# First row tiles loaded singly, their transposes evicted in halves, eleven dummy matmuls, D added on GpSimd, and a newly found order

## The chip, the cores and the metric

The kernel runs on one core of one Trainium2 chip. A core has five engines, each with its own queue of instructions: TensorE (PE in the profile; its weight loads are PEld), VectorE (DVE), ScalarE (ACT), GpSimd (POOL) and SyncE (SP), and 16 DMA engines that move data between the chip's memory and the core's two on-chip memories, SBUF and PSUM. TensorE writes only to PSUM; VectorE and ScalarE read it from there ("evict" it) into SBUF. The metric is the device time of one execution in microseconds (us), lower is better; a run's time is compared as a median over executions.

## What is computed

Inputs are bfloat16. The sequence has 2048 rows of 512 channels; the feed-forward width is 1792.

```
xn = layernorm(x)                                  # x = A_q, rows of 512
# branch A: a long convolution, written with FFTs in the reference
k_shift = 4-tap causal convolution of k along the rows
kv = k_shift * v
y  = causal convolution of kv with ssm_k, length 2048   # by FFT of length 4096
s  = xn * (y + kv * ssm_D)
# branch B: a gated feed-forward layer
h  = gelu(xn @ w_gate) * (xn @ w_up)
g  = silu(h @ w_down)
out = x + s * g
```

Since y + kv * D is the convolution of kv with a filter whose element 0 is larger by D, the kernel adds D to row 0 of the filter.

## The kernel before

**Tiling.** Row r of the sequence is tile t = r mod 16 at partition r div 16, so a tile is 128 x 512 and there are 16 of them, in four quarters q of four tiles. The feed-forward branch goes by quarters: normalise the four tiles (`ln`), transpose them (`xn_transpose`; quarter 0 on TensorE, the others by a transposing DMA), then for each of 14 column blocks m the gate and up matmuls (`unit`, four contraction steps each, 512 columns), GELU on ScalarE, the product on VectorE into HT, and then `down`. Blocks m = 0 and 1 of quarter 0 are cut further: their matmuls go tile by tile (128 columns), so that they can start when tile 0 is transposed.

**The convolution** is a two-stage FFT as matmuls. The filter's four pieces (Hn) are transposed on TensorE (L916) and evicted into HTr; stage 1 of the filter (L959) and of kv (L950) use half of the array's rows, two matmuls side by side ("packed"); the middle stage (L1028) uses sixteen 32 x 32 pieces of the array side by side; the results go through DRAM (ZH, ZK, ZI) to be rearranged. The inverse ends in the matmuls of L1278.

**The order.** All work is put down as tasks, numbered as they are added (`Sched.add`, helpers `op`, `load`). Each has one or two engines that could do it, a duration and what it depends on. `SEQ` is a list of all task numbers; a task is emitted in that order, on its first engine, or on its second where the number has a `b` behind it. The order was found beforehand with the planner's durations, and the planner's landing times of the loads stand in `LAND` (in ns). `Sched.run` goes through the list, gives buffers and PSUM banks to the tasks, and the emission then puts semaphore waits where they are needed (`Trk`). So within each engine's queue the order is that of `SEQ`, and an instruction that waits holds up all those behind it on its engine.

**The start.** SyncE issues the loads in the order of `ORDER` (helper L614): x in two halves of two tiles each (`load_x0`), the first gate and up weights, D, the filter, and so on. Meanwhile TensorE runs `N_WARM` dummy matmuls on a constant (`warm_up`). Statistics of each tile (L849, L850) go on VectorE, the variance plus epsilon (L859 on ScalarE or L860 on VectorE), the power -1/2 on GpSimd (L862), and the normalisation on VectorE (L871). TensorE transposes a normalised tile (L892, four matmuls against the identity) into one PSUM bank, and one 128 x 512 copy evicts it into xnT (helpers L632 on ScalarE, L635 on VectorE); then the gate matmuls (helper L641) can start. D is added to row 0 of the filter by one 1 x 512 VectorE operation (`h_fold`, L930), after the filter's first-half evictions and before stage 1 of tile pair 0.

Of the kernel before, what the change touches and what calls it, by code (L numbers as in the profile page):

```python
# [24 lines left out]
N_WARM = 13  # L25
ORDER = "x00 x01 w0 D0 h0 w1 h1 h2 h3 s0 k0 w2 x1 k1 k2 w3 d0 d1 v0 v1 k3 v2 v3 x2 x3"
SEQ = (
# [22 lines left out]
)  # L50
NF_BANKS = 4
ISSUE = 470.0
LAND = {"x0_0": 3800, "h0": 8050, "x0_1": 4900, "D": 6750, "wg0": 5850, "wu0": 6700, "h1": 12450, "wg1": 9600, "wu1": 11100, "h2": 13800, "h3": 15150, "sk": 17800, "kh1": 19200, "kh113": 19400, "kz": 10800, "k0": 20600, "wg2": 22500, "wu2": 24050, "x1": 25400, "k1": 26750, "k2": 28100, "wg3": 29650, "wu3": 31200, "wd0": 33450, "wd1": 35700, "v0": 37050, "v1": 38400, "k3": 39750, "v2": 41100, "v3": 42450}
W_XT, W_SW, W_BK, W_BH, W_ZI, W_BI, W_ZK, W_MI, W_G1 = 765000, 735000, 667000, 688000, 274000, 714000, 690000, 329000, 150000
NC_PAIRS = 4
SMALL = 1.15 * 262144
# [1308 lines left out]
```

## Time and profile before

| what | us |
|---|---|
| median of three runs | 189.29 (189.12 to 190.32) |
| the profiled execution | 189.28 |
| its span, first to last instruction | 187.5 |
| TensorE, VectorE, ScalarE, GpSimd busy in it | 182.2, 164.8, 140.0, 12.9 |

The span lacks 1.78 us of the profiled execution's own time; that part lies before the first and behind the last instruction. A group's line in the profile gives the source line, engine, operation, what is written from what, the shapes, the count, the busy time with the mean duration in ns, and the idle time before it with what ended that. A matmul's duration reaches from its start to the arrival of its last result, so matmuls of a stream overlap in the records: their pace is read from starts, or from the chain of waits, which merges them.

### The profile page before, as it was taken

What the parts mean: (1) busy time and instruction counts of PE and PEld (TensorE: products, weight loads), DVE (VectorE), ACT (ScalarE), POOL (GpSimd) and SP (SyncE); (2) the same over time, 40 slices, a digit from 0 to 9 for tenths busy, and PEclk for the clock granted to TensorE, in tenths of its full rate; (3) what the DMA queues carried; (4) which work ended last, traced back from release to release, by engine and by line L of the source; (5) the groups of instructions that cost most, each with busy time, mean ns of one, the idle gap of its engine ahead of it and who ended that gap; (6) DMA issues with size and microseconds to landing.
All of it is one profiled execution on the core that took longest, in us unless ns stands there. A gap on an engine that the chain in (4) does not pass through costs nothing.

```text
span 187.5 us, 3669 instructions
## 1 busy us (share of the span) xinstructions
PE 182.2 (97%) x1451; PEld 80.5 (43%) x1459; DVE 164.8 (88%) x249; ACT 140.0 (75%) x193; POOL 12.9 (7%) x26
## 2 busy tenths in 40 slices
PE   8899999999999999999999999999999999999993
PEld 3585443444334344334434433434333334445552
DVE  6897999999999999969459999998899994468995
ACT  3766697898698979888878779888887863144961
POOL 4502304100000000020200000000000000000000
PEclk9999999999999999999999999999999999999999
DMA  5999999999938695777999991869327056699226
GB/s 156 352 404 299 373 374 377 394 404 245 326 87 330 225 337 212 241 260 241 290 268 261 352 343 65 298 229 334 108 111 277 0 168 217 228 325 385 83 101 235
DMA packets 38502, 48.37 MB, mean 258 GB/s; under 512 B 9427, under 2 KB 28119, under 8 KB 38486
## 3 DMA queue, kind: packets, MB, share of 16 engines
q1 hardware_dynamic: 31958, 39.76, 64.1%
q10 hardware_dynamic: 6528, 8.39, 12.6%
q8 instruction: 11, 0.18, 0.5%
q14 instruction: 5, 0.04, 0.1%
HBM read 27.39 MB, written 14.68 MB: 224 GB/s over the span
## 4 chain that ended last, share of the span: by engine, by line
PE 91%; DVE 3%; DMA 2%; ACT 1%; issue 1%; POOL 0%
PE psall L641 71%; PE psall L1224 6%; PE psall L1028 6%; PE psall L950 2%; PE psall L959 2%; PE psall L916 2%; PE psall L1278 2%; DMA X<-in_A_q_dram 2%; ACT BO L632 1%; DVE stats L849 1%; DVE KAC L1005 1%; PE psall L892 0%; DVE XN L871 0%; DVE XN L965 0%; DVE HT L1203 0%
## 5 line engine op out<-in xcount | busy, mean ns | idle before, releaser
L641 PE MATMUL psall<-xnT,Wu 128*128 128x512 bf16 (+1 forms) x248 | 56.5, 359 | 0.0
L641 PE MATMUL psall<-xnT,Wg 128*128 128x512 bf16 (+1 forms) x248 | 55.8, 359 | 0.0
L1194 ACT ACTIVATE GE<-psall 128x512 bf16<-128x512 f32 x54 | 31.9, 606 | 13.6 <-PE psall L641 11.1
L641 PE MATMUL psall<-Wd,HT 128*128 128x512 bf16 (+1 forms) x174 | 38.3, 367 | 0.8 <-issue 0.6
L1203 DVE TENSOR_TENSOR HT<-psall,GE 128x512 bf16<-128x512 f32 x43 | 29.3, 682 | 7.8 <-PE psall L641 7.5
L641 PEld LDWEIGHTS psall<-xnT,Wu 128*128 128x128 bf16 x248 | 22.5, 98 | 26.1 <-issue 2.3
L641 PEld LDWEIGHTS psall<-xnT,Wg 128*128 128x128 bf16 x248 | 21.8, 98 | 26.0 <-issue 3.2
L632 ACT ACTIVATE BO<-psall 128x1024 bf16<-128x1024 f32 x20 | 19.9, 1022 | 9.4 <-PE psall L1278 4.8
L641 PEld LDWEIGHTS psall<-Wd,HT 128*128 128x128 bf16 x182 | 16.3, 98 | 21.2 <-issue 3.9
L1131 DVE TENSOR_TENSOR HSW<-KB,HSW 128x2048 bf16<-128x2048 bf16 x16 | 19.3, 1218 | 1.9 <-ACT KB L632 1.9
L632 ACT ACTIVATE HSW<-psall 128x1024 bf16<-128x1024 f32 x15 | 15.2, 1024 | 2.4 <-PE psall L1028 2.1
L632 ACT ACTIVATE KB<-psall 128x1024 bf16<-128x1024 f32 x15 | 14.6, 1026 | 0.8 <-PE psall L1028 0.8
L1011 DVE TENSOR_TENSOR KAC<-KAC,KTM 128x2048 bf16<-128x2048 bf16 x12 | 14.6, 1217 | 0.0
L1009 DVE TENSOR_TENSOR KTM<-KK,SKB 128x2048 bf16<-128x2048 bf16 x12 | 14.6, 1215 | 0.0
L632 ACT ACTIVATE AST<-psall 128x1024 bf16<-128x1024 f32 x12 | 12.1, 1032 | 0.9 <-PE psall L950 0.8
L1224 PE MATMUL psall<-Wd,HT 128*64 128x512 bf16 (+1 forms) x112 | 12.5, 366 | 0.0
L862 POOL TENSOR_TENSOR mv<-mv,NHALF 128x1 f32<-128x1 f32 (+1 forms) x7 | 7.3, 1049 | 68.6 <-DVE mv L850 48.0
L1235 ACT ACTIVATE G<-psall 128x512 bf16<-128x512 f32 x12 | 7.1, 597 | 6.3 <-PE psall L641 6.3
L849 DVE BATCH_NORM_STATS2 stats<-X 128x6 f32<-128x512 bf16 x16 | 10.5, 675 | 0.5 <-DMA X<-in_A_q_dram 0.5
L632 ACT ACTIVATE XN<-psall 128x1024 bf16<-128x1024 f32 x9 | 9.2, 1028 | 1.1 <-PE psall L959 1.0
L1237 DVE SCALAR_TENSOR_TENSOR G<-G,psall 128x512 bf16<-128x512 bf16 x12 | 7.9, 682 | 2.3 <-ACT G L1235 2.3
L1131 DVE TENSOR_TENSOR KB<-KB,HSW 128x2048 bf16<-128x2048 bf16 x8 | 9.7, 1219 | 0.1
(91 smaller groups left out, 178.3 us busy)
## 6 DMA issues: line engine op xcount, KB each, us to landing
BH<-ZH SPq DMA_DIRECT2D x8, 512.0 KB, 5.0
HSW<-HSW SPq DMA_DIRECT2D x16, 256.0 KB, 3.7
BK<-ZK SPq DMA_DIRECT2D x8, 512.0 KB, 5.9
ZI<-BO ACTq DMA_DIRECT2D x16, 256.0 KB, 2.8
BI<-ZI SPq DMA_DIRECT2D x8, 512.0 KB, 8.5
ZK<-AST SPq DMA_DIRECT2D x6, 512.0 KB, 2.9
ZH<-XN ACTq DMA_DIRECT2D x5, 512.0 KB, 4.3
Hn<-in_A_ssm_k_dram SPq DMA_DIRECT2D x4, 512.0 KB, 8.0
```

Of the source, the lines that this page charges most:

```text
L632: return h.activation(o, i, ACTF.Copy, scale=scale)
L641: return h.matmul(o, lhsT=l, rhs=r, start=st, stop=sp)
L849: t_stats[t] = op([("DVE", 670.0)], lambda e, h, t=t: h.bn_stats(stats[:, t, :], X[:, t, :]), r=[bX[q][t % 4]], w=[bst[t]], rr=[R_X[t]], w ...
L862: t_pw = op([("POOL", 2500.0 if q else 600.0)], lambda e, hd, ts=ts, n=n: hd.tensor_tensor(mv[:, ts, 3:4], mv[:, ts, 2:3], NHALF[:, 0:n, : ...
L1009: op([("DVE", dur)], lambda e, h, j=j, m=m: h.tensor_tensor(KTM[:, m.slot, :, :], kk(j), sk(j), ALU.mult), r=need + [bSKB[j], a], w=[m], r ...
L1011: op([("DVE", dur)], lambda e, h, m=m: h.tensor_tensor(KAC[:, a.slot, :, :], KAC[:, a.slot, :, :], KTM[:, m.slot, :, :], ALU.add), r=[m], ...
L1028: trk.op("PE", lambda h: h.matmul(ps(s, i)[b, :], lhsT=wt(col)[a, :], rhs=data(col)[a, :], start=n < 16, stop=n >= len(todo) - 16, tile_po ...
L1131: return hd.tensor_tensor(pair(KB, *(2 * DM * z for z in slots())) if to else x, k, x, ALU.mult)
L1194: op([("ACT", act(512))], lambda e, h: h.activation(GE[:, g.slot, :], bank(pg), ACTF.Gelu_apprx_tanh), r=[pg], w=[g], rr=lambda: R_bank(pg ...
L1203: op([("DVE", dve(512, 1))], lambda e, h: h.tensor_tensor(HT[:, q % 2, m, :], bank(pu), GE[:, g.slot, :], ALU.mult), r=[pu, g], w=[bHT[q][m]],
L1224: trk.op("PE", lambda h, m=m, i=i, c=c: h.matmul(pc()[c, :], lhsT=HT[:, q % 2, m, 128 * jt + 64 * i:128 * jt + 64 * i + 64], rhs=Wd[:, m, ...
L1237: op([("DVE", dve(512, 1))], lambda e, h, g=g, pc=pc: h.scalar_tensor_tensor(out=g, in0=g, scalar=1.0, in1=pc(), op0=ALU.add, op1=ALU.mult ...
```

## The change

Five things change together.

- The first load of x, two tiles at once, is split into two loads of one tile each; the second pair stays one load. `ORDER` has one entry more.
- The transposes of tiles 0 and 1 go to two PSUM banks each, two of the four 128-column pieces in each, and are evicted by two copies of 128 x 256, for which either engine can be chosen (`N_SPLIT = 2`). The matmuls that read a tile wait for both halves.
- There are 11 dummy matmuls instead of 13.
- D is added by GpSimd instead of VectorE.
- `SEQ` is a new order of all tasks (812 instead of 809: one load and two evictions more), with new choices of engines, and `LAND` and one planner duration (ScalarE's variance, 240 to 300) are new.

```diff
-N_WARM = 13
-ORDER = "x00 x01 w0 D0 h0 w1 h1 h2 h3 s0 k0 w2 x1 k1 k2 w3 d0 d1 v0 v1 k3 v2 v3 x2 x3"
+N_WARM = 11
+ORDER = "x00 x01 x02 w0 D0 h0 w1 h1 h2 h3 s0 k0 w2 x1 k1 k2 w3 d0 d1 v0 v1 k3 v2 v3 x2 x3"
 SEQ = (
...
-LAND = {"x0_0": 3800, "h0": 8050, "x0_1": 4900, "D": 6750, "wg0": 5850, "wu0": 6700,
...
+LAND = {"x0_0": 3450, "h0": 8200, "x0_1": 4300, "x0_2": 5100, "D": 6850, "wg0": 5900, "wu0": 6750,
...
+N_SPLIT = 2
...
         def load_x0(t):
-            ts = slice(*((0, 2), (2, 4))[t])
+            ts = slice(*((0, 1), (1, 2), (2, 4))[t])
...
-            pp = [B(f"psxn{q}_{j}", pX) for j in range(4)]
             for j in range(4):
...
+                pieces = [(0, 2), (2, 4)] if j < N_SPLIT else [(0, 4)]
+                pp = [B(f"psxn{q}_{j}" + "b" * (k0 > 0), pX) for k0, _ in pieces]
+
+                def tr(e, j=j, pieces=pieces, pp=pp):
+                    for (k0, k1), p in zip(pieces, pp):
+                        for kd in range(k0, k1):
+                            o = bank16(p)[:, 128 * (kd - k0):128 * (kd - k0 + 1)]
+                            trk.op("PE", lambda h, o=o, kd=kd: h.transpose(o, XN[:, 4 * q + j, 128 * kd:128 * (kd + 1)], ident[:]), r=[R_XN[4 * q + j], R_id], w=R_bank(p), accum=True)
+                S.add([("PE", 4 * 66.0)], tr, r=[bid, bXN[4 * q + j]], w=pp, lat=150.0)
+                for (k0, k1), p in zip(pieces, pp):
+                    def ev(e, h, j=j, k0=k0, k1=k1, p=p):
+                        return copy(e, h, xnT[:, q, j, k0:k1, :].rearrange("p k c -> p (k c)"), bank16(p)[:, 0:128 * (k1 - k0)])
+                    n = 128 * (k1 - k0)
...
-        h_fold = op([("DVE", 420.0)], lambda e, h: h.tensor_tensor(HT0, HT0, Drow[:], ALU.add),
+        h_fold = op([("POOL", 1200.0)], lambda e, h: h.tensor_tensor(HT0, HT0, Drow[:], ALU.add),
```

The start of the new order, as names (VectorE's tasks of the first tiles): statistics of tiles 0, 1, 3, normalise 0, normalise 1, the second half of tile 0's eviction, statistics of tile 2, the first half of tile 1's eviction, normalise 3, normalise 2. Before, they were: statistics 0 and 1, normalise 0, statistics 2, normalise 1, statistics 3, normalise 2, normalise 3. ScalarE now does the variance of tiles 0, 1 and 3 and two half evictions before it computes the sines of the table (`m_sin`); before, it did the variance of tile 0 and then `m_sin`. TensorE, after the dummies, transposes tiles 0 and 1 and then runs the eight groups of blocks m = 0 and 1 on them; before, it put block work on tile 0 between the transposes of tile 1 and those of the filter.

More of the change, by code (lines that the diff above doesn't have):

```diff
@@ L547, in build_kernel @@
         R_xnT = [[res(f"xnT{b}_{j}", xnT[:, b, j, :, :]) for j in range(4)] for b in range(2)]
+        R_xnT0 = [[res(f"xnT0_{j}_{k}", xnT[:, 0, j, 2 * k:2 * k + 2, :]) for k in range(2)] for j in range(N_SPLIT)]
         R_GE = [res(f"GE{j}", GE[:, j, :]) for j in range(3)]
@@ L650, in build_kernel @@
         bxnT = [[B(f"xnT{q}_{h}") for h in range(4 if q < 1 else 1)] for q in range(NQ)]
+        bxnT0 = [[B(f"xnT0_{j}" + "b" * k) for k in range(2)] for j in range(N_SPLIT)]
         bF1, bG1, bMF, bMI, bid, bSKB = B("F1"), B("G1"), B("TF"), [B(f"MI{i}") for i in range(2)], B("id"), [B(f"SKB{j}") for j in range(4)]
@@ L860, in var @@
                     return hd.tensor_scalar(mv[:, ts, 2:3], mv[:, ts, 1:2], LN_EPS, None, ALU.add)
-                t_var = op([("DVE", 180.0)] + ([] if q else [("ACT", 240.0)]), var, r=[bconst, bF1, *bm], w=[be], rr=rm + [R_ep], ww=rm)
+                t_var = op([("DVE", 180.0)] + ([] if q else [("ACT", 300.0)]), var, r=[bconst, bF1, *bm], w=[be], rr=rm + [R_ep], ww=rm)
                 t_pw = op([("POOL", 2500.0 if q else 600.0)], lambda e, hd, ts=ts, n=n: hd.tensor_tensor(mv[:, ts, 3:4], mv[:, ts, 2:3], NHALF[:, 0:n, :], ALU.pow),
@@ L886, in xn_transpose @@
                 return
-            pp = [B(f"psxn{q}_{j}", pX) for j in range(4)]
             for j in range(4):
-                def tr(e, j=j):
-                    for kd in range(KD):
-                        o = bank16(pp[j])[:, 128 * kd:128 * (kd + 1)]
-                        trk.op("PE", lambda h, o=o, kd=kd: h.transpose(o, XN[:, 4 * q + j, 128 * kd:128 * (kd + 1)], ident[:]), r=[R_XN[4 * q + j], R_id], w=R_bank(pp[j]), accum=True)
-                S.add([("PE", 4 * 66.0)], tr, r=[bid, bXN[4 * q + j]], w=[pp[j]], lat=150.0)
-            for j in range(4):
-                def ev(e, h, j=j):
-                    return copy(e, h, xnT[:, q, j, :, :].rearrange("p k c -> p (k c)"), bank16(pp[j])[:, 0:512])
-                xnT_tasks.append(op([("ACT", act(512)), ("DVE", dve(512, 2))], ev, r=[pp[j]], w=[bxnT[q][j]],
-                   rr=lambda j=j: R_bank(pp[j]), ww=[R_xnT[q][j]]))
+                pieces = [(0, 2), (2, 4)] if j < N_SPLIT else [(0, 4)]
[10 more added lines that the diff above has]
+                    n = 128 * (k1 - k0)
+                    xnT_tasks.append(op([("ACT", act(n)), ("DVE", dve(n, 2))], ev, r=[p], w=[bxnT[q][j]] if n == 512 else [bxnT0[j][k0 // 2]],
+                       rr=lambda p=p: R_bank(p), ww=[R_xnT[q][j]] if n == 512 else [R_xnT0[j][k0 // 2]]))
         d_out = []
@@ L1189, in unit @@
                 return
-            tg = S.add([("PE", pe(4))], half(pg, Wg, "g"), r=[bW["g"][ci]] + bxnT[q], w=[pg], lat=150.0)
-            tu = S.add([("PE", pe(4))], half(pu, Wu, "u"), r=[bW["u"][ci]] + bxnT[q], w=[pu], lat=150.0, after=[tg])
+            tg = S.add([("PE", pe(4))], half(pg, Wg, "g"), r=[bW["g"][ci]] + (bxnT[q] if q else [*bxnT[q][N_SPLIT:], *sum(bxnT0, [])]), w=[pg], lat=150.0)
+            tu = S.add([("PE", pe(4))], half(pu, Wu, "u"), r=[bW["u"][ci]] + (bxnT[q] if q else [*bxnT[q][N_SPLIT:], *sum(bxnT0, [])]), w=[pu], lat=150.0, after=[tg])
             gu_tasks[q] += [tg, tu]
```

4 lines of the change are left out of this document (2 added, 2 removed), and 44 rows, old and new, of the table SEQ.

## The prediction

> **What bounds the kernel now.** I read the first part of the page, the busy time by stretch, the chain of waits and TensorE's own waits, and last the timeline of the first 8 us.
>
> ```profile
> PE 182.2 (97%) x1451; PEld 80.5 (43%) x1459; DVE 164.8 (88%) x249; ACT 140.0 (75%) x193; POOL 12.9 (7%) x26
> ```
> ```profile
> core 0: us, PE busy (x) PEld busy (x) DVE busy (x) ACT busy (x) POOL busy (x), PEclk, DMA share, GB/s
> 0.00:6.30 6.30, 5.54 (x13) 1.75 (x13) 4.61 (x19) 3.10 (x5) 3.17 (x16) 1.00 0.67 206
> ...
> 20.00:24.00 4.00, 3.69 (x22) 1.79 (x19) 4.00 (x7) 2.21 (x4) 0.25 (x1) 1.00 1.08 385
> ...
> 40.00:100.00 60.00, 59.58 (x358) 23.75 (x359) 53.15 (x81) 50.88 (x71) 2.03 (x2) 1.00 0.84 260
> 100.00:146.00 46.00, 45.84 (x510) 18.20 (x510) 44.41 (x51) 38.49 (x51) 0.00 (x0) 1.00 0.68 235
> ...
> 184.00:187.50 3.50, 0.60 (x11) 0.42 (x8) 1.31 (x5) 0.55 (x2) 0.00 (x0) 0.93 0.55 186
> ```
> ```profile
> PE psall L641 <- PEq L1350: 0.8, 1, 0.8
> PE psall L641 <- issue: 0.6, 4, 0.2
> PE psall L892 <- DVE XN L871: 0.5, 1, 0.5
> PE psall L959 <- DVE HT L1203: 0.3, 1, 0.3
> ```
> In the second fence the columns are the length of the stretch and each engine's busy time in it; in the third, who waited for whom, the sum, the count and the longest. TensorE is busy in 97% of the span, and all its waits before the last matmul add up to 2.2 us: 0.8 before the program starts, 0.5 in front of the second tile's transposes, 0.3 in front of an L959 matmul, 0.6 without a cause. A busy TensorE need not be a full one, so the chain is read for its pace:
>
> ```profile
> 7.24 0.40 PE psall L892 x4
> 7.63 1.16 PE psall L641 x20
> ...
> 18.38 2.70 PE psall L641 x12
> ...
> 24.91 5.18 PE psall L641 x24
> ...
> 59.72 0.54 PE psall L950 x4
> ```
> Twenty-four 512-column matmuls in a row take 5.18 us, 0.216 each; twelve of them between two packed groups (L959 and L950 use half of the array's rows) take 2.70 and not 2.59, and four packed ones, two pairs side by side, 0.54 and not 0.43. So going into packed mode and out again costs 0.11 us each way. From 7.24 us on the chain is almost all TensorE. The kernel is bound by TensorE's work; only the start (the first 7.5 us), the number of mode changes, a few small waits, and the tail of 3 us can give time. VectorE stands right behind: full from 20 to 24 us, 44.41 of 46 us from 100 to 146.
>
> **The change, part by part.** The rows of the start:
>
> ```profile
> 0.72 0.87 SPq L614 DMA_DIRECT2D X<-in_A_q_dram  x2
> ...
> 1.64 0.43 SPq L614 DMA_DIRECT2D Wg<-in_B_w_gate_dram  x1
> ...
> 3.92 0.69 DVE L849 BATCH_NORM_STATS2 stats<-X 128x6 f32<-128x512 bf16 x1 [0.52 <-DMA X<-in_A_q_dram]
> ...
> 4.65 0.18 DVE L850 BATCH_NORM_AGGREGATE mv<-stats 128x2 f32<-128x6 f32 x1
> ...
> 4.86 0.29 ACT L859 ACTIVATE mv<-mv,EPSC 128x1 f32<-128x1 f32 x1 [1.88 <-DVE mv L850]
> ...
> 5.24 1.21 POOL L862 TENSOR_TENSOR mv<-mv,NHALF 128x1 f32<-128x1 f32 x2 [2.29 <-ACT mv L859]
> ...
> 5.85 0.41 DVE L871 TENSOR_SCALAR XN<-X,mv 128x512 bf16<-128x512 bf16 x1
> 6.18 0.69 DVE L849 BATCH_NORM_STATS2 stats<-X 128x6 f32<-128x512 bf16 x1
> ...
> 6.32 0.40 PE L892 MATMUL psall<-ident,XN 128*128 128x128 bf16 x4
> ...
> 6.78 0.40 DVE L871 TENSOR_SCALAR XN<-X,mv 128x512 bf16<-128x512 bf16 x1
> ...
> 6.87 0.58 ACT L632 ACTIVATE xnT<-psall 128x512 bf16<-128x512 bf16 x1
> ...
> 7.50 0.40 PE L641 MATMUL psall<-xnT,Wg 128*128 128x128 bf16 x4
> ```
> *Loads.* The first transfer halves to 128 KB. Its landing is bounded by 0 (the time is latency) and 0.59 us earlier (131 KB at the rate below); I take 0.35, landing at 3.55, which is also the step in the planner's own table (3800 to 3450). One load more is one issue more on SP's queue, 0.43 us (half of 0.87), and every load behind it is issued that much later.
>
> ```profile
> 1.50:2.50 1.00, 1.00 (x4) 0.37 (x3) 0.90 (x7) 0.51 (x1) 0.89 (x6) 1.00 0.64 221
> ```
> ```profile
> Wg<-in_B_w_gate_dram SPq DMA_DIRECT2D x1, 256.0 KB, 4.0
> ```
> The first gate weights, issued at 1.64, land 4.0 us later, at 5.6; they are first used at 7.50, so 0.43 is covered with 1.4 to spare. Without that cover it would cost its 0.43 in full.
>
> *Normalisation of the first two tiles.* Read against the order in which the program adds its tasks, the lists of numbers are lists of names. VectorE's new order is: statistics of tiles 0, 1 and 3, normalise 0, normalise 1, half evictions. With the durations above (an operation starts up to 0.08 before the last one's end, as 6.18 against 5.85 + 0.41): statistics of tile 0 from 3.57 to 4.26, aggregate to 4.48, statistics of tile 1 from 4.42 to 5.10, of tile 3 from 5.22 to 5.90, normalise 0 from 5.84. That is where it is now: the 0.35 won is spent on the statistics moved in front. Normalise 1 follows at 6.30, not 6.78 (aggregate 1 done at 5.30, ScalarE 0.29, GpSimd 0.58, rounding and hand-overs 0.1). So both tiles' transposes lie before 7.2, in time that TensorE has free.
>
> *Evictions in halves.*
> ```profile
> L635 DVE COPY HTr<-psall 128x1024 bf16<-128x1024 bf16 x4 | 2.8, 689 | 1.1 <-PE psall L916 1.0
> ...
> L632 ACT ACTIVATE HTr<-psall 128x1024 bf16<-128x1024 bf16 x2 | 2.0, 1021 | 0.1
> ...
> L632 ACT ACTIVATE xnT<-psall 128x512 bf16<-128x512 bf16 x3 | 1.8, 593 | 0.2 <-PE psall L892 0.2
> ...
> L635 DVE COPY xnT<-psall 128x512 bf16<-128x512 bf16 x1 | 0.4, 425 | 0.1
> ```
> From 1024 to 512 columns ScalarE saves 0.43 and VectorE 0.26, so a half of 256 takes about 0.38 and 0.29. Tile 0's halves run side by side: ScalarE's, the later, ends at 6.87 + 0.38 = 7.25, and the first gate matmul starts at 7.30 instead of 7.50. Tile 1's halves end by 8.0, before tile 0's sixteen matmuls do (0.06 each from the x20 row, 7.30 + 0.9), so no hole opens. **Front: -0.20 us.** If the first tile lands no earlier, the same sums give a first gate matmul at 7.65, a loss of 0.15; if it lands 0.59 earlier, tile 3's statistics hold the rest, a gain of 0.3.
>
> *Two dummies fewer.* They end at 0.76 + 11 x 0.427 = 5.46 instead of 6.3, in front of work that can't start before 6.3: nothing gained, and a risk told below.
>
> *D added on GpSimd.*
> ```profile
> 17.35 2.90 POOL L986 COPY SKB<-SKR 128x512 bf16<-128x512 bf16 x4 [8.09 <-DMA SKR<-in_A_shift_k_dram]
> ...
> 17.53 1.06 DVE L930 TENSOR_TENSOR HTr<-HTr,Drow 1x512 bf16<-1x512 bf16 x1
> ...
> 30.62 3.06 POOL L862 TENSOR_TENSOR mv<-mv,NHALF 128x4 f32<-128x4 f32 x1 [10.38 <-DVE mv L860]
> ```
> VectorE loses 1.06 us. GpSimd's price is not in the trace: bounds are 0.73 (a copy of 512 columns, 2.90 / 4) and 3.06 (a power on few elements beside a busy VectorE). I take 1.2, nearer the copy. It is queued behind the four copies of L986, which wait for a load, so it ends 0.73 to 3.06 after their end at 20.25, by 23.3; its one reader, stage 1 of tile pair 0, comes in the new order after some 24 us of matmuls counted from 7.3, at about 31. Behind it on GpSimd stands only the second quarter's power, needed at about 31 too. Covered at either bound: 0.
> What does VectorE gain? The trace has the 1 x 512 addition at 1.06, longer than a 512-column product from PSUM at 0.67, and it overlaps the L986 copies. By the Trainium skill ("SBUF — State Buffer", the section on which operations contend) a VectorE operation with two SBUF inputs and a GpSimd operation that reads SBUF exclude each other; by that rule the addition on GpSimd can hold up VectorE's next operation by its whole length, and VectorE would gain about nothing. The rows agree in direction.
>
> *The new order.* It has 78 mode changes instead of 80, since two packed groups are joined: **-0.22 us**. It also hands VectorE evictions that ScalarE had: one of 1024 columns more in the inverse stage, one U tile (512 columns), one more of the filter's transposes, two halves.
> ```profile
> L635 DVE CAST XN<-psall 128x1024 bf16<-128x1024 f32 x1 | 1.2, 1202 | 0.0
> ...
> L1203 DVE TENSOR_TENSOR HT<-psall,GE 128x512 bf16<-128x512 f32 x1 | 0.7, 666 | 0.0
> ```
> 1.20 + 0.67 + 0.69 + 0.58 less the 1.06 is 2.1 us more on VectorE, not less. From 40 to 146 it has 8.4 us free, so I take 0, with the other end below. The wait of 0.3 before L959 sits in a different sequence now; I leave it in.
>
> **Sum.** The profiled execution took 189.28 us (span 187.5 and 1.78 around it), the median of the runs is 189.29. 189.28 - 0.20 - 0.22 = 188.86, so 188.9; with the front's bounds, and the 0.3 in or out, 188.4 to 189.3.
>
> **Rivals.**
> *A, VectorE's relief counts.* VectorE is full from 20 to 24 us, and there TensorE waits 0.3 for it. If the 1.06 us free that stretch, and the tail, which has one VectorE product less after the last matmuls of the inverse transform have begun, gains as much, the time is 188.9 - 0.3 - 0.3 = 188.3. Against it: the 2.1 us handed to VectorE, and the shared access.
> *B, the clock is released late.*
> ```profile
> L641 PE MATMUL psall<-const-bfloat16-1.0 x13: 527/631/631, 0.8 to 5.8; 128*128 128x512 bf16 x13
> ```
> Dummies start every 0.43 us, twice 0.216: half pace, though the granted clock reads 1.00. Only the shortest (527 against 631) can hold the change, so full pace came in the last one, near 6.2, after 5.4 us of uninterrupted work. The new dummies end at 4.7 us of work, and TensorE then idles 0.85 us. If a moment decides, nothing is lost; if the missing 0.7 us must be made up by real work at half pace, 0.35; if the count starts anew at 7.30, 5.4 us at half pace cost 2.7. The mean of the last two is 1.5: 190.4, slower than now. It decides when the first transposes or gate matmuls run at 0.11 us each and not 0.056. The Trainium skill ("TensorE: Matmul & The Clock Gate", Part 1) has a free-running window of about 3.4 us whose activity sets the clock; by it the next decision after 6.2 comes by 9.6, the loss is at most (9.6 - 7.3) / 2 = 1.15, an estimate, and the time 190.0. That full pace came late in an unbroken run agrees with it.
> *C, VectorE becomes the bound.* From 100 to 146 it has 1.6 us free and gets 1.2 more; if its free moments are waits for data that can't be filled, the U tile and the 1024 columns push what TensorE waits for (PSUM banks, HT) by 0.67 + 1.20: 188.9 + 1.9 = 190.7, also slower. It decides once that stretch shows VectorE full and TensorE below 45.8 of 46.
> *D, the split does nothing* (landing at 3.90, no earlier): 189.28 + 0.15 - 0.22 = 189.2, inside the forecast's range.
>
> **How the numbers follow.** Forecast with D 0.45, A 0.15, B 0.17, C 0.23. The time is the forecast's, 188.9. The range goes down to A (188.2, leaving out some 0.08 of a better tail) and up past C to 190.9, leaving out about 0.11: dearer forms of B and C. One per cent is 1.9 us, about what a measurement of this kernel tells from no change: 187.4 and 191.2. Below 187.4 would need more than every wait named here: 0.03. Above 191.2 lies C with more than one engine late, or B's dear end: 0.12. Within: 0.85.
>
> **What would show it.** First statistics near 3.55, second normalisation near 6.3, first gate matmul near 7.3 (front right); gate matmuls of 128 columns at 0.06 us each (B wrong); the addition on GpSimd ending well before its reader, no wait on it (D's cover right); TensorE's waits after 7.3 still near 1 us (C wrong). I am wrong if a wait of over 0.5 us appears inside the body, or if the last matmul ends later than 184.6 with the front on time.

## The result, and the profile after

| | median of the runs, us | range, runs | profiled execution, its span |
|---|---|---|---|
| before | 189.47 | 188.71 to 190.32, 22 | 189.28, 187.5 |
| changed | 190.62 | 189.68 to 195.66, 22 | 190.55, 188.7 |

The changed kernel takes 1.0052 times the time of before (95% interval 1.0037 to 1.0067): 1.0 us longer where 0.4 us less was forecast. The ratio leaves out executions more than 1.5% above the fastest of their kernel (five of the changed kernel's 22, from 192.56 up), so it says a little less than the medians, which lie 1.15 apart. In the changed kernel, TensorE's waits (who waited for whom: sum in us, count, longest), the engines' busy times and two of the stretches are:

```profile
PE psall L966 <- ACT XN L634: 0.8, 1, 0.8
PE psall L643 <- PEq L1357: 0.8, 1, 0.8
PE psall L923 <- DMA Hn<-in_A_ssm_k_dram: 0.6, 1, 0.6
PE psall L898 <- DVE XN L874: 0.5, 1, 0.5
PE psall L643 <- issue: 0.2, 1, 0.2
PE psall L643 <- ACT GE L1201: 0.2, 1, 0.2
```
```profile
PE 182.3 (97%) x1449; PEld 80.1 (42%) x1457; DVE 167.0 (88%) x251; ACT 137.8 (73%) x192; POOL 13.3 (7%) x27
```
```profile
core 0: us, PE busy (x) PEld busy (x) DVE busy (x) ACT busy (x) POOL busy (x), PEclk, DMA share, GB/s
...
40.00:100.00 60.00, 58.82 (x351) 23.39 (x354) 53.34 (x81) 48.70 (x70) 2.12 (x2) 1.00 0.87 259
100.00:146.00 46.00, 46.00 (x510) 18.08 (x509) 44.70 (x50) 39.94 (x52) 0.00 (x0) 1.00 0.71 239
```

Two waits are new: 0.6 us for the filter's first piece (Hn, a DMA) and 0.8 us for an eviction by ScalarE (L634). TensorE has lost 0.8 us of its busy time from 40 to 100 us, and none from 100 to 146. The timeline of the start (TensorE's rows, then VectorE's, the first numbers being start and length):

```profile
0.76 4.85 PE L643 MATMUL psall<-const-bfloat16-1.0 128*128 128x512 bf16 x11 [0.76 <-PEq L1357]
6.13 0.93 PE L898 MATMUL psall<-ident,XN 128*128 128x128 bf16 x8 [0.52 <-DVE XN L874]
6.94 0.39 PE L643 MATMUL psall<-xnT,Wg 128*128 128x128 bf16 x4
...
9.49 0.69 PE L923 MATMUL psall<-ident,Hn 128*128 128x128 f32 x4 [0.58 <-DMA Hn<-in_A_ssm_k_dram]
```
```profile
3.49 0.69 DVE L852 BATCH_NORM_STATS2 stats<-X 128x6 f32<-128x512 bf16 x1
...
5.68 0.93 DVE L874 TENSOR_SCALAR XN<-X,mv 128x512 bf16<-128x512 bf16 x2
```

The first tile is there early, the first gate matmul starts at 6.94 and not 7.50, and yet the last group of the kernel starts later (184.87; before, 183.64):

```profile
184.87 0.95 PE L643 MATMUL psall<-Wd,HT 128*128 128x128 bf16 x14
```
```profile
183.64 0.95 PE L641 MATMUL psall<-Wd,HT 128*128 128x128 bf16 x14
```

To see where the 0.56 us of the front and 1.23 more went, I took for groups of matmuls TensorE's **lag**: the start of the group less the duration of all TensorE work ahead of it in its order (0.0555 us for 128 columns, 0.216 for 512, 0.11 for a mode change). Where the lag rises, TensorE has stood still or run slowly. Up to its last group TensorE has 175.28 us of work before and 175.06 changed: the 0.22 us of mode changes are there.

```
lag, us             first gate  near 25   near 42   near 90   last group
before                    7.06     7.39      7.42      7.53         8.36
changed                   6.50     7.30      7.90      8.99         9.81
changed, again            7.04     7.09      8.12      8.36         9.57
two loads                 6.80     6.67      7.67      7.91         9.19
GELU first                6.71     7.29      7.91      8.94         9.79
combined                  6.89     7.24      7.68      8.33         9.16
combined, front           6.73     7.88      8.32      8.57         9.39
before, x split           6.51     8.57      8.57      8.70         9.52
before, 9 dummies         7.01     9.43      9.43      9.56        10.39
```

(The lower rows are experiments, below. A step can be read to about 0.1 us.) The changed kernel starts 0.56 ahead, and that is gone by 25 us; it loses some 0.6 near 31 to 42 and 1.06 at 52. The 0.8 after 90 us is the same before, and no listed wait goes with it: from 100 to 146 us TensorE is busy for 45.84 of 46 us before and for 46.00 changed.

### The profile page after: what moved, and what is told of

It is laid out like the page before. It is cut to its first block, busy times and chain, and to the rows that moved or that the text cites. A ratio compares the mean times of both kernels' runs of the same rounds, so it can differ in the third digit from the quotient of the medians.

```text
span 188.7 us, 3668 instructions
## 1 busy us (share of the span) xinstructions
PE 182.3 (97%) x1449; PEld 80.1 (42%) x1457; DVE 167.0 (88%) x251; ACT 137.8 (73%) x192; POOL 13.3 (7%) x27
## 4 chain that ended last, share of the span: by engine, by line
PE 86%; DMA 6%; ACT 2%; DVE 2%; SPq 1%; issue 1%
PE psall L643 66%; PE psall L1231 6%; PE psall L1035 6%; DMA Hn<-in_A_ssm_k_dram 3%; DMA ZH<-XN 3%; PE psall L923 2%; PE psall L957 2%; PE psall L966 2%; PE psall L1285 2%; SPq L616 1%; ACT XN L873 1%; DVE KAC L1012 1%; ACT XN L634 1%; DVE HT L1210 0%; DVE G L1253 0%
## 5 line engine op out<-in xcount | busy, mean ns | idle before, releaser
L1210 DVE TENSOR_TENSOR HT<-psall,GE 128x512 bf16<-128x512 f32 x43 | 28.8, 683 | 5.4 <-PE psall L643 5.0
L643 PEld LDWEIGHTS psall<-xnT,Wu 128*128 128x128 bf16 x248 | 21.7, 98 | 27.6 <-issue 4.3
L634 ACT ACTIVATE BO<-psall 128x1024 bf16<-128x1024 f32 x19 | 18.8, 1023 | 8.7 <-PE psall L1035 4.6
L634 ACT ACTIVATE HSW<-psall 128x1024 bf16<-128x1024 f32 x15 | 14.9, 1025 | 4.2 <-PE psall L1035 4.1
L634 ACT ACTIVATE KB<-psall 128x1024 bf16<-128x1024 f32 x15 | 14.8, 1026 | 1.8 <-PE psall L1035 1.6
L634 ACT ACTIVATE AST<-psall 128x1024 bf16<-128x1024 f32 x10 | 10.1, 1024 | 2.1 <-PE psall L957 2.0
L865 POOL TENSOR_TENSOR mv<-mv,NHALF 128x1 f32<-128x1 f32 (+1 forms) x7 | 6.4, 915 | 65.9 <-DVE mv L853 51.6
L634 ACT ACTIVATE XN<-psall 128x1024 bf16<-128x1024 f32 x10 | 10.0, 1019 | 0.9 <-PE psall L966 0.8
```

What stands on the lines that cost most here:

```text
L634: return h.activation(o, i, ACTF.Copy, scale=scale)
L643: return h.matmul(o, lhsT=l, rhs=r, start=st, stop=sp)
L1210: op([("DVE", dve(512, 1))], lambda e, h: h.tensor_tensor(HT[:, q % 2, m, :], bank(pu), GE[:, g.slot, :], ALU.mult), r=[pu, g], w=[bHT[q][m]],
```

## The experiments

Times of all of them, each against runs of the kernel before on the same chip:

| | run | median, us (range, runs) | ratio to before, 95% |
|---|---|---|---|
| e0 | changed, again | 191.02 (190.34 to 192.3, 9) | 1.0067, 1.0035 to 1.0099 |
| e1 | changed, two loads | 190.13 (189.48 to 194.25, 12) | 1.0020, 1.000 to 1.004 |
| e2 | changed, 13 dummies | 191.15 (189.51 to 196.14, 12) | 1.0065, 1.0036 to 1.0095 |
| e3 | changed, D on VectorE | 190.62 (189.75 to 192.28, 12) | 1.0056, 1.0027 to 1.0084 |
| e4 | changed, start filled | 190.74 (189.61 to 192.03, 12) | 1.0061, 1.0037 to 1.0084 |
| e5 | changed, 52 us filled | 192.12 (191.24 to 193.06, 6) | 1.0132, 1.0101 to 1.0163 |
| e7 | changed, GELU first | 190.3 (189.77 to 194.87, 12) | 1.0032, 1.001 to 1.0054 |
| e8 | e1 and e7 | 190.46 (188.91 to 194.23, 12) | 1.0037, 1.001 to 1.0065 |
| e9 | before, x split by tiles | 189.99 (189.32 to 190.87, 12) | 1.0019, 0.9997 to 1.0042 |
| e10 | before, 11 dummies | 190.2 (188.88 to 190.77, 12) | 1.0024, 0.9997 to 1.0051 |
| e11 | e8 with 13 dummies | 189.57 (189.07 to 191.47, 12) | 0.9994, 0.9961 to 1.0026 |
| e12 | before, x split by rows | 191.11 (189.52 to 191.58, 12) | 1.0070, 1.0045 to 1.0094 |
| e13 | before, 9 dummies | 190.43 (189.42 to 191.34, 12) | 1.0050, 1.0031 to 1.0069 |
| e14 | e11, start reordered | 189.91 (189.36 to 195.88, 12) | 1.0022, 0.9995 to 1.0049 |
| e15 | before, an issue more | 190.18 (189.42 to 190.83, 10) | 1.0040, 1.0024 to 1.0056 |
| e16 | before, 1 KB pieces | 189.66 (189.24 to 191.37, 12) | 1.0030, 1.0006 to 1.0054 |

### The third load of x

> The changed kernel unaltered, beside its variants. All theories expect what was measured: about 190.6 us, 1.005 of the kernel before, with some runs of 192 to 196. In its trace TensorE should again wait about 0.6 us for the first piece of the filter near 9 us and about 0.8 us for a ScalarE eviction near 51 us.

> The changed kernel with x's first four tiles in two loads again; its order, dummies, halves and the addition of D stay. Theory L (the loads: the third issue and the smaller pieces make all loads behind late, and with them the filter's first piece and the stores and loads near 45 us): the filter's first piece lands at 8.1 to 8.6 us instead of 9.4, the wait near 51 us shrinks too, and the time is 189.5 or less. Theory O (the order: it leaves TensorE nothing to do at two places): the start loses about 0.4 us, the wait near 9 us goes, both about cancel, the wait near 51 us stays, 190.3 to 190.9.

```diff
         def load_x0(t):
-            ts = slice(*((0, 1), (1, 2), (2, 4))[t])
+            if t == 1:
+                S.add([("loads", ISSUE)], lambda e: None, nbytes=1, land=float(LAND["x0_1"]))
+                return
+            ts = slice(*((0, 2), None, (2, 4))[t])
```

The second profile of the changed kernel (e0, 190.34 us) did not repeat the two new waits: neither the wait for the filter's piece nor the one for ScalarE's eviction is there. Its first gate matmul came at 7.48, because tile 3's statistics, which the new order puts early, waited for the third load:

```profile
5.61 0.69 DVE L852 BATCH_NORM_STATS2 stats<-X 128x6 f32<-128x512 bf16 x1 [0.42 <-DMA X<-in_A_q_dram]
```

With the front only 0.02 us ahead, the filter's piece, landed at 8.75, held nobody. What the two traces share is the loss from 31 to 42 us (1.0 here).

With tiles 0 and 1 in one load again (e1) the changed kernel gains 0.9 us against e0 (190.13 and 191.02, same batch), 0.6 by the ratios of e1 and of the first measurement, with intervals that just overlap; no other single part gives as much. Its lag near 25 us is 6.67, 0.6 less than the changed kernel's. Does the load cost by itself, or only in the new order?

> The kernel before with one thing of the change alone: its first load of x (tiles 0 and 1) is split into two loads of one tile each, so that there is one issue more on SyncE's queue; order, evictions, dummies and the addition of D are those of before. Theory L0 (the third load of x costs time wherever it stands, since everything behind it lands later): 0.5 to 0.9 us slower than before, 190.0 to 190.4, with a new wait of TensorE in the first 15 us. Theory L1 (the third load costs only together with the new order, which has nothing left to run when the filter's first piece is late): in the order of before the filter's first piece has 1.9 us of slack (landing near 8.1, first used near 10), so the time stays within 0.3 of before, 189.2 to 189.8, no wait longer than before's 0.5 at the start, and the loads behind x land 0.4 to 1.3 later without anyone waiting.

```diff
-            load(f"x0_{t}", X[:, ts, :], ...
+            for i, s in ((0, sem), (1, sem2)):      # t == 0: tiles 0 and 1, one issue each
+                dma("SP", X[:, i:i + 1, :], x_dr[:, i:i + 1, :], s, [], [R_X[i]])
```

The timeline of TensorE in this run, with the order of before:

```profile
6.95 0.40 PE L641 MATMUL psall<-xnT,Wg 128*128 128x128 bf16 x4
...
8.01 0.39 PE L641 MATMUL psall<-xnT,Wg 128*128 128x128 bf16 x4
10.11 0.69 PE L924 MATMUL psall<-ident,Hn 128*128 128x128 f32 x4 [1.71 <-DMA Hn<-in_A_ssm_k_dram]
```

The first gate matmul is 0.55 us earlier than before, and then TensorE stands for 1.71 us before the filter's transposes. From 25 us to the end its lag is about 1.2 above that of the kernel before (9.52 and 8.36 at the last group), and the execution took 190.45, 1.17 more. The theory that only the new order suffers (L1) doesn't fit this trace. The medians put the cost at 0.5 us, with an interval that just reaches zero. What makes it late, the issue or the shorter pieces of the transfer (1 KB a row of a tile, 2 KB for two tiles)?

> The kernel before with its first load of x split into two loads in another way: rows 0 to 63 of the core's memory in one and 64 to 127 in the other, both tiles in each. So there are as many issues as with the split by tiles (three for x), but each piece that is moved stays 2 KB long, where the split by tiles has pieces of 1 KB. Theory I (the extra issue, 0.47 us, holds back all loads behind it): as with the split by tiles, the filter's first piece comes late, with a wait of TensorE for it of 1 us or more, and the time is near 190.0. Theory P (short pieces lower the rate at which the first loads arrive): the rate from 4 to 6 us is back at some 310 to 335 GB/s instead of 236, the filter's first piece lands near 8.6 (0.47 later than in before) against its use near 8.6 to 8.8, so a wait of 0.2 at most, and the time is within 0.3 of before.

> The kernel before with one issue more on SyncE's queue and nothing else: a row of 1 KB of x's last tile is loaded between x's two loads (and overwritten with the same values by its own load later). Pieces of x's loads stay 2 KB. In the runs so far the kernels with two loads moved 308 to 334 GB/s from 4 to 6 us and the filter's first piece landed at 8.1 to 9.6 us (median 8.8); those with x split by tiles moved 222 to 281 GB/s, and it landed at 8.8 to 10.1 (median 9.5). Theory I (the issue): the rate falls below 290 as well, and the piece lands near 9.5. Theory P (short pieces): the rate stays at 308 to 334 and the piece lands 0.45 later than with two loads, since it is issued 0.45 later; 189.5 to 189.9.

> The kernel before with two loads for x's first four tiles as it has, but tiles 0 and 2 in the first and 1 and 3 in the second, so that each piece moved is 1 KB long instead of 2, with the same bytes and the same issues. Theory P (short pieces): 222 to 281 GB/s from 4 to 6 us, the filter's first piece (issued at 3.1) lands at 9 or later, and the time is 189.8 to 190.3 (part of it from tile 1's statistics, which now wait for the second load). Theory I (the issue): 308 to 334 GB/s, the piece lands at 8.1 to 8.8, and only tile 1's statistics come later.

```diff
+    # e12, in place of the first load: for ps in (0:64, 64:128)
+    dma("SP", X[ps, 0:2, :], x_dr[ps, 0:2, :], sem, [], [r])
+    # e15, behind the first load
+    dma("SP", X[0:1, 15, :], x_dr[0:1, 15, :], sem2, [], [R_X[15]])
-            ts = slice(*((0, 2), (2, 4))[t])
+            ts = slice(t, 4, 2)    # e16
```

| | filter's first piece: issued, landed | GB/s, 4 to 6 us | TensorE's wait for it |
|---|---|---|---|
| before | 3.10, 8.1 | 334 | none |
| e15, an issue more | 3.35, 9.5 | 274 | 1.0 |
| e16, 1 KB pieces | 3.24, 8.6 | 295 | none |
| e9, both | 3.58, 10.0 | 236 | 1.7 |
| changed | 3.58, 9.4 | 269 | 0.6 |

In e15 nothing but a 1 KB load was added, and the row of the wait is there:

```profile
9.58 0.69 PE L924 MATMUL psall<-ident,Hn 128*128 128x128 f32 x4 [1.05 <-DMA Hn<-in_A_ssm_k_dram]
```

Theory P (short pieces alone) falls as the cause of the wait: pieces of 2 KB with one issue more bring it, and e15's time is clear of the kernel before's (1.0024 at least); 1 KB pieces without the issue do not, though they lower the rate too, and e16's trace ends level with the kernel before's (last group at 183.60). With one issue more, the piece is issued 0.25 to 0.48 us later and lands 1.2 to 1.9 later; why the early rate falls with it I can't tell from these traces. These are single traces, and the landing scatters: 8.1 to 9.6 in the eight traces with two loads for x's first four tiles, 8.75 to 10.1 in the ten with three. e12 told nothing of this: its half-height loads were slow in themselves (x's three issues took 1.85 us instead of 1.35, VectorE's first statistics started at 4.71), and what followed belongs to the dummies, below.

### Filling the holes

> The changed kernel with one alteration of the order: the transposes of row tiles 3 and 2 come before the first transposes of the filter, not behind them. Theory O: the 0.6 us wait near 9 us is filled with their 0.45 us; if nothing later takes it back the time falls by 0.4 us to about 190.2, if the stall near 45 to 51 us is set by transfers it takes all of it back and the time stays at 190.6. Theory L: 190.6, the late loads hold the rest.

> The changed kernel with one alteration of the order: near 50 us the second halves of stage 1 of the filter's tile pairs 7 and 4 come behind two groups of down matmuls (2.2 us of TensorE's work) instead of in front of them. Theory O: the wait near 51 us, and the 1.0 us by which TensorE falls behind its work there, go: 189.6, and the runs of 192 to 196 go if they are the same wait at its worst. Theory L: the stores are late whatever stands there, and the wait moves behind the two groups with at least half its size: 190.1 or more.

```diff
-  ... htr0_0 xtr2 xtr3 ...          # e4, order of tasks on TensorE
+  ... xtr3 xtr2 htr0_0 ...
-  ... s1H7_1 s1H4_1 (two groups of down matmuls) ...     # e5
+  ... (two groups of down matmuls) s1H7_1 s1H4_1 ...
```

With tiles 3 and 2 transposed ahead of the filter (e4) the wait for the filter's piece is gone, and the lag goes on to 9.02 near 42 us and 10.09 at the end: other waits, the first for VectorE's eviction of the filter (0.5), take the place. e5 made it worse. In its trace the stores took 5.0 and 4.6 us, so the wait that it was to fill would not have come (see the next part); the two packed groups set back made ScalarE's evictions late, and kv's stage 1 (L957) waited for them, 1.0 and 0.4 us. Neither hole was closed by putting other work in front.

### The new order from 31 to 55 us

> The changed kernel with one alteration of ScalarE's order: near 33 us a GELU of quarter 0 stands in front of the first normalisations of quarter 1, which wait for GpSimd's power (3.06 us), not behind them. Theory N (those waiting normalisations hold the GELUs, and so PSUM banks and TensorE: the 0.8 to 1.0 us that TensorE falls behind between 31 and 42 us in every trace of the changed order): 190.2 to 190.5. Rival (the quarter's x load, or VectorE, is what is late there): 190.8 to 191.2.

```diff
-  ... norm4 ... gelu0_10 ...        # order of tasks on ScalarE
+  ... gelu0_10 norm4 ...
```

ScalarE's, TensorE's and GpSimd's rows of the changed kernel that this part is about; the bracket says how long the engine had been idle, and for what:

```profile
34.06 1.52 ACT L873 ACTIVATE XN<-X,NB__69,mv 128x512 bf16<-128x512 bf16 x2 [0.67 <-DVE NB__69 L869]
35.49 0.57 ACT L1201 ACTIVATE GE<-psall 128x512 bf16<-128x512 f32 x1
...
49.36 1.02 ACT L634 ACTIVATE X<-psall 128x1024 bf16<-128x1024 f32 x1 [3.01 <-PE psall L643]
50.55 1.02 ACT L634 ACTIVATE XN<-psall 128x1024 bf16<-128x1024 f32 x1 [0.16 <-DMA ZH<-XN]
```
```profile
51.63 0.39 PE L966 MATMUL psall<-HTr,F 64*128 64x512 bf16 x2 [0.80 <-ACT XN L634]
```
```profile
31.17 1.93 POOL L865 TENSOR_TENSOR mv<-mv,NHALF 128x4 f32<-128x4 f32 x1 [8.54 <-DVE mv L863]
```
```profile
ZH<-X ACTq DMA_DIRECT2D x1, 512.0 KB, 6.2
ZH<-XN ACTq DMA_DIRECT2D x1, 512.0 KB, 5.7
```

The kernel before, at the same two places:

```profile
33.44 0.60 ACT L1194 ACTIVATE GE<-psall 128x512 bf16<-128x512 f32 x1 [1.02 <-DVE HT L1203]
33.93 1.51 ACT L870 ACTIVATE XN<-X,NB__69,mv 128x512 bf16<-128x512 bf16 x2
```
```profile
ZH<-X ACTq DMA_DIRECT2D x1, 512.0 KB, 4.2
ZH<-XN ACTq DMA_DIRECT2D x1, 512.0 KB, 4.0
```

In the new order the second quarter's normalisation stands in ScalarE's queue ahead of a GELU. It waits for its bias (NB, which hangs on GpSimd's power), and the GELU, whose bank TensorE needs, waits behind it. Before, a GELU stood in front and covered that wait. With one GELU moved (e7) ScalarE has the same idle 0.68 but does the GELU first; the median is 190.3 against 190.62 (e3) and 191.15 (e2) of the same batch, so some 0.3 to 0.8, with intervals that overlap.

The traces say when that helps. The power took either 1.93 or 3.06 us, as in e0:

```profile
30.99 3.06 POOL L865 TENSOR_TENSOR mv<-mv,NHALF 128x4 f32<-128x4 f32 x1 [7.95 <-DVE mv L863]
```

With the normalisation in front, the lag rises between 35 and 39 us by some 0.75 where the power took 3.06 (e0, e1, e3, e4, e5) and by 0.35 where it took 1.93 (the changed kernel, e2). With the GELU in front it rises by 0.3 to 0.35 either way (3.07 in e11; 1.93 in e7, e8 and e14). So in these traces the move takes the 0.4 that a slow power costs, and nothing else: between the profiled executions of the changed kernel and of e7 TensorE's rows that both traces have from 32 to 42 us start within 0.01 of each other. The other 0.35, and 0.1 to 0.2 more near 41 us, are in all eleven traces of the new order and not in that of the kernel before; no run takes them away, and their cause stays open.

The second place is the filter's stage 1 near 50 us. An eviction into X or XN may start only when the store that reads that place (ZH, to DRAM) has landed. The store from X was issued at 43.08 and landed 6.2 us later, at 49.28; the eviction into X started at 49.36, 1.2 us after the packed matmuls in front of it had ended (47.55 and 0.60). The bracket of that row names a matmul, but the row of e7, the same but for 0.06 us, names the store:

```profile
49.30 1.02 ACT L634 ACTIVATE X<-psall 128x1024 bf16<-128x1024 f32 x1 [2.95 <-DMA ZH<-X]
```

The eviction into XN follows behind, held 0.16 us more by its own store, and TensorE's next packed matmuls wait 0.8 for it. This wait is there in the traces of the changed kernel and of e7, and twice in e8 (0.77 and 0.90), where the store from X took 6.1 to 6.9 us; it is absent in the other eight traces of the new order, where it took 3.9 to 5.0. So it is a loss of some executions. Whether the new order makes the store slow is not shown: there is one trace of the unaltered kernel before, with 4.2.

### D on GpSimd

> The changed kernel with D added on VectorE again, at the same place of the order. If the move to GpSimd relieved VectorE, 1.06 us come back on VectorE near 23 us and the time rises by 0.3 to 1 us from 191.0. If the two engines' operations exclude each other, or VectorE has room there, the time stays within 0.2 us: 190.8 to 191.2.

```diff
-        h_fold = op([("POOL", 1200.0)], ...
+        h_fold = op([("DVE", 1200.0)], ...
```

No difference from the changed kernel in time (1.0056 and 1.0052). GpSimd's addition took 1.15 us (1.6 to 1.7 in the nine other traces that have it there) and ended at 22.6, eight before its reader; beside it, VectorE's addition of two SBUF tiles took 1.67 us. In e3, where the fold is VectorE's own (1.22), that addition took 0.67.

```profile
21.48 1.15 POOL L937 TENSOR_TENSOR HTr<-HTr,Drow 1x512 bf16<-1x512 bf16 x1
```
```profile
21.51 1.67 DVE L972 TENSOR_TENSOR XN<-XN 128x1024 bf16<-128x1024 bf16 x1
```
```profile
21.53 1.22 DVE L937 TENSOR_TENSOR HTr<-HTr,Drow 1x512 bf16<-1x512 bf16 x1
...
23.24 0.67 DVE L972 TENSOR_TENSOR XN<-XN 128x1024 bf16<-128x1024 bf16 x1
```

So VectorE saves 1.22 us and loses 1.00 of it again. By the Trainium skill ("SBUF — State Buffer", on which operations contend) a VectorE operation with two SBUF inputs and a GpSimd operation that reads SBUF exclude each other; the trace agrees, with 1.67 beside GpSimd's addition and 0.67 without.

### The dummies

> The changed kernel with 13 dummies again, nothing else. Theory B (the clock): the dummies' end 0.85 us before the real work costs time in some runs or in all; then the median falls by 0.4 us or more from 191.0 and the runs of 192 and more grow rare. Rival: the first transposes and gate matmuls ran at full pace in all five traces so far, the dummies do nothing; 190.6 to 191.2.

> The kernel before with 11 dummy matmuls instead of 13, all else unchanged. Theory B (fewer dummies let the clock be released late in some executions): the median moves by less than 0.3, but some executions are 1 us or more longer and start their gate matmuls at 0.107 us each instead of 0.056. Rival (dummies do not matter): the spread of the executions is that of before, 188.7 to 191.3, and first gate and transposes run at 0.056.

> The kernel before with 9 dummy matmuls. With 11, 5 of 12 executions had a mean granted clock of 0.989 to 0.990 and a median of 190.52, the other 7 (0.998 or more) a median of 189.44; with 13, all 29 beside them had 0.998 or more. Theory B (the fewer the dummies, the more often the clock is taken down once in the execution): more than half of the executions show 0.99 or less, the median rises to 190.5 or above, and if the profiled execution is one of them, a stretch of matmuls at half pace can be seen in it. Rival (the share has nothing to do with the count): 0 to 5 of 12, median 189.4 to 190.2.

```diff
-N_WARM = 11
+N_WARM = 13    # e2, on the changed kernel
-N_WARM = 13
+N_WARM = 11    # e10, on the kernel before (9 in e13)
```

In e2 nothing: another wait follows at the start anyway (1.3 us for the filter). In the kernel before the count does matter. Of e10's 12 executions, seven have a mean granted clock of 0.998 or more and a median of 189.44, as before; five have 0.989 or 0.990 and a median of 190.52. All 140 executions of the kernel before in these batches have 0.997 or more. With 9 dummies six of 12 fall, and the profiled one, which reads 1.00, shows the other form of it:

```profile
0.76 4.00 PE L641 MATMUL psall<-const-bfloat16-1.0 128*128 128x512 bf16 x9 [0.76 <-PEq L1350]
6.13 0.61 PE L892 MATMUL psall<-ident,XN 128*128 128x128 bf16 x4 [1.37 <-DVE XN L871]
...
7.45 0.63 PE L641 MATMUL psall<-xnT,Wg 128*128 128x128 bf16 x4
7.87 0.63 PE L641 MATMUL psall<-xnT,Wu 128*128 128x128 bf16 x4
...
12.57 0.64 PE L916 MATMUL psall<-ident,Hn 128*128 128x128 f32 x4
13.04 0.61 PE L641 MATMUL psall<-xnT,Wu 128*128 128x128 bf16 x8
```

Groups of four start 0.43 us apart, 0.107 a matmul instead of 0.056, until 12.6. The lag rises from 7.01 to 9.43: 2.4 us. e8's trace (11 dummies; this execution took 192.14, above its set's median) has the same until 9.9 us, for 1.2 us. And e12, with 13 dummies but x later, shows the clock that was released and taken back, in the column of the granted clock (PEclk, third from the right):

```profile
core 0: us, PE busy (x) PEld busy (x) DVE busy (x) ACT busy (x) POOL busy (x), PEclk, DMA share, GB/s
6.00:8.00 2.00, 0.40 (x4) 0.23 (x4) 1.89 (x7) 1.97 (x4) 1.66 (x3) 1.00 1.01 318
8.00:10.00 2.00, 1.97 (x21) 1.93 (x22) 1.36 (x6) 0.84 (x2) 1.06 (x2) 0.58 0.97 341
10.00:12.00 2.00, 2.00 (x20) 1.94 (x19) 0.41 (x1) 0.88 (x2) 0.05 (x1) 0.57 1.09 400
```

TensorE had been idle for 1.35 us before its first transposes at 7.11. So the count alone doesn't decide, since e12 has 13: six of its 12 executions fall, and two of e16's 12, also with 13. Nor does the length of the pause behind the dummies alone: it is 0.64 in e10's trace (five of 12) and 0.34 in e16's, and 0.83 and 0.84 in those of e15 and e11, which have 13 dummies and none of 22. Fewer dummies (e10, e13) and x later (e12) both went with more executions that fall; by which rule stays open.

The moment at which the dummies themselves reach full pace is not fixed either. Their starts come 0.22 us apart instead of 0.43 after some 3.0 us of dummies in e7 and e15, after 3.4 in e4, and only in the last one, after 5.4, in the kernel before.

The longest executions are something else. Thirteen executions of the new order, in six of its eleven sets, took 193.5 to 196.1 us, and none of the kernel before or its variants did. Three of them have 13 dummies (e2, e14). All thirteen have a mean granted clock of 0.980 to 0.991, but none was profiled, so their cause stays open.

### The parts put together

> Two loads of x again and the GELU in front of the normalisations, both at once; the rest as changed. If the two losses are separate (0.9 us of the third load, 0.6 to 0.8 of the GELU's place) the time is 189.3 to 189.6, no slower than the kernel before; if one contains the other, 190.0 to 190.3.

> The changed kernel with three parts taken back: tiles 0 and 1 in one load again, the GELU of block 10 ahead of the second quarter's last normalisation on ScalarE, and 13 dummies. Theory S (the losses lie in three separate places: the start, the stretch from 31 to 42 us, and the stores near 45 to 53 us): the first two are taken back, the third varies by run, so 189.3 to 189.9, with TensorE's lag behind its work at the first gate near 6.7, 7.2 near 42 us. Rival N (what one part gives back the next wait takes, as when a hole at the start was filled before): 190.1 to 190.5, as each part alone gave.

> The changed kernel with tiles 0 and 1 in one load, the early GELU and 13 dummies (the version that came out at 189.57), and VectorE's and TensorE's order at the start set for tile 0: both halves of its eviction ahead of the second normalisation, tile 3's statistics behind that, two groups of gate and up matmuls ahead of tile 1's transposes. Theory S (places add up): first gate matmul near 7.0 instead of 7.33, TensorE's lag 0.3 less from there to the end, 189.2, below both kernels. Rival N (the next wait takes it: filter piece, or the transposes of tiles 2 and 3, now later): lag back at 7.2 by 17 us, 189.5.

```diff
-  norm0 norm1 ... stats3 ahead of norm0, xtr0 xtr1 g0_1_j0 u0_0_j0      # e11, start
+  norm0 ev_xT0 norm1 stats3 ..., xtr0 g0_1_j0 u0_0_j0 xtr1              # e14
```

e8 and e11 differ in the dummies alone: 1.0037 and 0.9994, on different chips and with intervals that overlap. e8's profiled execution shows the half pace (its lag goes from 7.02 to 8.26 at the filter's transposes) and five of its 12 executions a clock near 0.99; e11 has none. e11 takes back three parts (the load, the GELU, the dummies) and is level with the kernel before; the halves and the rest of the order were not taken back one by one. Its waits have neither the filter's piece nor the ZH store:

```profile
PE psall L901 <- DVE XN L877: 0.8, 1, 0.8
PE psall L643 <- PEq L1360: 0.8, 1, 0.8
PE psall L960 <- DVE V L1023: 0.4, 1, 0.4
PE psall L643 <- ACT GE L1204: 0.2, 1, 0.2
PE psall L643 <- issue: 0.2, 1, 0.2
```

e14 started the gate matmuls at 6.95 instead of 7.33, after 0.41 us for tile 0's eviction, and then stood for about 0.3 in the up matmuls and 0.34 for the filter's piece: its lag near 25 us is 0.6 higher. No version came out ahead of the kernel before.

## Why the prediction was wrong

The median, 190.62, lies in the range (188.2 to 190.9), but the forecast, 188.9, had the wrong sign. That the range holds it is luck: its upper part was there for rival C, and C did not happen. By its steps:

**The front, -0.20.** Right in kind. In the profiled execution the first statistics are at 3.49 (forecast 3.55), the second normalisation near 6.1 (6.3), the first gate matmul at 6.94 (7.30): -0.56. In the six other traces of this start (e0, e2 to e5, e7) that matmul is at 7.14 to 7.48, -0.36 to -0.02, so the size was about right and scatters.

**"so 0.43 is covered with 1.4 to spare": the first step that failed.** It was worked out for the gate weights, and they were indeed in time (in e7's trace the up weights held TensorE for 0.17). The extra issue also stands in front of the filter's first piece, whose first use was 0.5 us behind its landing in the kernel before (8.63 and 8.1). The front moved that use forward and the issue moved the landing back, by 1.2 and not 0.4. e9 and e15 show the wait by itself. e1, with the issue taken out, gives back 0.6 to 0.9. Nor did the sum ask when the third load lands, which brings tile 3: it started tile 3's statistics at 5.22, and in e0 they waited until 5.61.

**The two dummies, "nothing gained, and a risk".** The risk is real. Rival B had the place (gate matmuls at 0.11 each) and the prices: 1.2 us in e8's trace, and 2.4 in e13's (9 dummies), near the upper end of 2.7. By the window of the Trainium skill ("TensorE: Matmul & The Clock Gate", Part 1) the prediction had put the loss at 1.15 at most, an estimate; e8's 1.2 is close to that, e13's 2.4 is twice as much. The 5.4 us of work from which B was reckoned is what one trace showed; in others full pace came after 3.0. The profiled execution of the changed kernel isn't one of these (its gate groups start 0.23 apart), so its loss is not B's. e10 shows B alone, as a share of the executions.

**D on GpSimd, 0.** Right: 1.15 us in the profiled execution (1.2 assumed; 1.6 to 1.7 in others), covered, and with no effect; the doubt whether VectorE gains was right too.

**The new order.** The 0.22 of two mode changes is there in the work. VectorE's 2.1 us more came as 2.2 (167.0 against 164.8) and did no harm: rival C is wrong, TensorE is busy for 46.00 of 46 us in the stretch that was to decide it. **What failed is the 0 for everything else in the order.** I priced the order by sums over VectorE and by mode changes, and not by what now stands in front of what on ScalarE: all seven traces of this order without the move lose 0.5 to 1.1 of lag from 31 to 42 us. Of that, the normalisation ahead of a GELU is 0.4 where GpSimd's power is slow; the remaining 0.5 has no cause that a run shows. The test named beforehand, a wait of over 0.5 us inside the body, is what appeared, at 52 us: an eviction that waited for a store of 6.2 us. It was priced at nothing; that it is the order's doing is not shown, since eight traces of the new order lack it.

**The sum, as measured in the profiled execution** (e0's adds up from other places). Front -0.56; wait for the filter +0.77 of lag; 31 to 42 us +0.6; the store +1.06; work -0.22; less the 0.36 that the kernel before loses from its first gate matmul to 42 us as well: 1.3, against 1.27 between the two profiled executions (190.55 and 189.28).

## What to carry to other kernels

When a load is split, follow every transfer behind it in the queue to its first use, not the next one alone; a front that starts earlier needs its second operand earlier too. Price a new order by what stands ahead of each short operation that the bounding engine waits for, on every engine's queue: busy sums don't show it. Work that holds an engine's clock up is safest when it lasts until the real work starts (none of 140 executions fell), and one profile does not show what its absence costs: look at the spread of the executions. Profile a kernel twice before a wait is called its own.

## What the runs showed of the hardware

- One load of 1 KB between others (e15) went with the issue of a 512 KB transfer 0.25 us later and its landing 1.3 later; the core moved 274 GB/s from 4 to 6 us instead of 334. All kernels with two loads for x's first four tiles in 2 KB pieces showed 308 to 334 there (seven traces), those with three 222 to 282 (ten).
- The column of the granted clock reads 1.00 while matmuls run at half pace before the clock has first been released (e13, to 12.6 us), and 0.50 when it is taken back later (e12, from 8.4 to 11.6 us; 0.57 and 0.58 in the two-microsecond stretches above, which are only partly at half pace). A mean of 0.99 in a run is the second form: 3.4 us at half pace in 189 are 0.009.
- Four microseconds of dummies in a row (e13) did not release the clock, while three were enough in e7 and e15 and 5.4 were needed in the kernel before; a pause of 1.35 us behind 13 of them preceded its being taken back (e12).
- GpSimd's power on 128 x 4 elements took either 1.93 us (five traces of the new order) or 3.06 to 3.07 (the other six, and all seven of the old order), and nothing between; what decides it is open.
